# Strassen's seven products for the first product of a two-layer mixture, with both products interleaved

## The chip, the cores and the metric

The kernel runs on one core of one Trainium2 chip. The metric is the device time of one execution in microseconds, the median of several. Below, PE is the engine that does the matmuls (with PEld its weight loads), DVE the vector engine, ACT the scalar engine, POOL the GpSimd engine, and SP the engine whose queue issues most of the DMAs. L123 is line 123 of the kernel before.

## What is computed

The reference is float32 throughout: a gated linear attention, then a first mixture without routing, then a second one over E = 4 experts. N is 3072 tokens, the model width is 384, the hidden width F = 1024.

```
a = x @ w1;  b = x @ w2;  x1 = ((a * b) @ w3) @ w_out          # first mixture
p = probs / (probs.sum(-1, keepdims=True) + 1e-09)
for e in range(4):                                             # second mixture
    h = maximum(x1 @ W1[e], 0)                                 # first product,  384 -> 1024
    out += p[:, e:e+1] * (h @ W2[e])                           # second product, 1024 -> 384
```

The change is in the second mixture and in the loads that prepare it.

## The kernel before

**Float32 from three matmuls.** Each float32 operand is split into a high part, rounded to float32r, and a low part, the rest. `mm3` (L45) makes a product of three matmuls into one PSUM bank: high with high, low with high, high with low. The high part is an ACT copy, the low part a subtraction on POOL or DVE (`split`, L52).

**First stage (attention and first mixture).** A planner (`Plan`, L316) takes every piece of work with an engine, a cost, a due number and the pieces it depends on, and calls the pieces in the order of a modelled clock: of the pieces that are ready on an engine, the one with the lowest due number goes first. That gives each engine a fixed program order, and on the chip each engine works through its own in order. The planner knows only the dependencies it is told of. The tile framework adds the waits that buffers need: the first instruction that writes a new tile waits until the tile that had the slot before has been read for the last time, wherever these reads stand in the other engines' orders.

Eight token tiles of 384 go through the first mixture. For the last two tiles the PE's order is: x1 of tile 6 (72 matmuls, three results), then the products `a` and `b` of tile 7 (16 results, `products`, L633), then x1 of tile 7 (`moe`, L688). All these results use one pool of three PSUM banks (`pmm`, L415), in turn. An x1 result is copied out by ACT (`evac`, L733), an `a` result by ACT (`copy_a`, L654), a `b` result by DVE, which multiplies it with the copy of `a` (`mult`, L658). While tile 7 is at work, the planner also places the first weights of the second mixture: `opened` (L894) is the point at which the attention's memory is free, after the products of tile 6; from there eight loads `wload` (L865), with their splits on ACT and POOL, chained by explicit dependencies on the buffers they reuse.

**Second mixture.** After the planner, the order is written out by hand. For each expert e and each of six tiles of 512 tokens: for each of eight blocks f of 128 hidden units, nine matmuls of 512 columns (three blocks of the width, `mm3` each) make h in a PSUM bank (`hps`, four banks); ACT takes relu and the high part out of the bank, DVE the low part (L987, L988). One step later follow twelve matmuls of 384 columns (`outs`, L971: four groups of 128 tokens), which add this block's part of the second product to four accumulators in PSUM (`ops`). After the eighth block DVE adds p times the accumulators to `acc` in SBUF, and for the last expert they go to DRAM. Weight loads and the splits of x1 for the next tile (POOL) are generators in a list `side`; `tick` (L939) advances each by one step after each f. `check_words` (L120) is a test of the raw weights of the first mixture, with DMAs of about 1 MB and three ACT passes for each of 17 pieces.

Of the kernel before, what the change touches and what calls it, by code (L numbers as in the profile page):

```python
# [402 lines left out]
def gated_attention_moe_kernel(tc, qT, kT, aT, vP, w1, w2, w3T, wo, probs, ew, out):  # L403
# [4 lines left out]
    with tc.manual_schedule(), root:  # L408
# [216 lines left out]

        ab_done = {}
        x1_use = {}
        wts = {}
        conv_done = {}
        g_lo = {}  # L630
# [57 lines left out]
        def moe(j):  # L688
# [24 lines left out]
            for m, (d, f0, f1) in enumerate(((0, 0, 3), (0, 3, 6), (1, 0, 3), (1, 3, 6), (0, 6, 8), (1, 6, 8),  # L713
                                             (2, 0, 3), (2, 3, 6), (2, 6, 8))):
                def unit(d=d, f0=f0, f1=f1):
                    if f0 == 0:
                        us["x", d] = pmm.tile([128, 512], F32, tag="mm", name="xps")[:, :TT]
                    for f in range(f0, f1):
                        s = slice(d * 128, (d + 1) * 128)
                        gg = tiles["g", j, f]  # L720
                        mm3(nc, us["x", d], wts[2, 0][:, f, s], wts[2, 1][:, f, s], gg[:, 0], gg[:, 1],
                            f == 0, f == KF - 1)

                deps = [prev] + [g_lo[j, f] for f in range(f0, f1)]
                if f0 == 0:
                    slots[d] = []
                prev = add("PE", 3 * (f1 - f0) * MM, due + UNIT_DUE * (16 + m), unit, w3_done, deps,
                           bank=slots[d] if f0 == 0 else None)
                if d == KD - 1:
                    for f in range(f0, f1):  # L730
                        x1_use[j, f] = prev
                if f1 == KF:
                    def evac(d=d):  # L733
                        x1 = tiles["x1"]() if callable(tiles["x1"]) else tiles["x1"]
                        A.activation(out=x1[:, d, j * TT:(j + 1) * TT], in_=us["x", d], func=ACTF.Copy)  # L735
                    slots[d].append(add("ACT", act(TT), due + UNIT_DUE * (16 + m), evac, prev, pre_done))


        pre = []
# [117 lines left out]
        add("DVE", 1.0, 3 * TILE_DUE, norm_p, add("SP", 0.5, 2 * TILE_DUE, load_p))  # L857


        slots = {}  # L860
        n_raw = [0]
        wraw = []
        epool = None

        def wload(n):  # L865

            e, f = divmod(n, KF)
            slots[n] = []
            rs = []
            for u in range(2):  # L870
                r = wraw[n_raw[0] % len(wraw)]
                n_raw[0] += 1
                nc.sync.dma_start(out=r, in_=ew[u][e, f])
                if n % 12 < 8:
                    w = epool.tile([128, 2, TT], F32R, tag="ws", name="ws", bufs=16)
                else:
                    w = mpool.tile([128, 2, TT], F32R, tag="gg", name="wg", bufs=KF)
                slots[n].append(w)
                rs.append(r)
            yield  # L880
            yield
            for u in range(2):
                yield from split(nc, slots[n][u][:, 0], slots[n][u][:, 1], rs[u])

        def open_e():
            att_s.close()
            nonlocal epool
            epool = root.enter_context(tc.tile_pool(name="e", bufs=1, side="right"))
            t = mpool.tile([128, 6, TT], F32, tag="xt", name="wraw", bufs=2)
            wraw.extend(t[:, i] for i in range(6))  # L890

        att_all = [d for n in at.values() for d in n.values()]
        j = NTILE - 1
        opened = add("SP", 0.0, j * TILE_DUE, open_e, att_all, ab_done[j - 1])  # L894
        freed = []
        for n in range(8):
            due = j * TILE_DUE + WL_STEP * n
            gen = {}

            def step(n=n, gen=gen):  # L900
# [12 lines left out]
            freed.append(prev)  # L913

        xsb = []

        def xsplit(n):
            t = n % NT2
            return split(nc, xsb[n % 2][:, 0], xsb[n % 2][:, 1], x1[:, :, t * T2:(t + 1) * T2])

        def x_hi():
            xsb.extend(wtile([128, 2, KD, T2], F32R, "xs") for _ in range(2))
            tiles["xsplit"] = xsplit(0)
            next(tiles["xsplit"])

        def x_lo():
            finish(tiles["xsplit"])
# [5 lines left out]
        hb = wtile([128, 3, 2, T2], F32R, "hb")  # L933
        ps1.close()


        side = []

        def tick():  # L939
            for g in list(side):  # L940
                if next(g, side) is side:
                    side.remove(g)

        acc = [wtile([128, 8, DM], F32, "acc") for _ in range(NR // 8)]
        pho = root.enter_context(tc.tile_pool(name="ph", bufs=4, space=PSUM))
        poo = root.enter_context(tc.tile_pool(name="po", bufs=4, space=PSUM))
        wraw += [mpool.tile([128, TT], F32, tag=t, name="wraw", bufs=2) for t in "aagg"]
        n_raw = [0]
        late = list(range(8, 12))
# [4 lines left out]
        n_test = B * NCH  # L954

        def held_out():
            ps = pho.tile([128, T2], F32, tag="h", name="fps")[0:1, 0:1]
# [4 lines left out]
        nxt = 12  # L962
        nh = 0
        for e in range(E):
            for t in range(NT2):
                n = e * NT2 + t
                x = xsb[n % 2]
                ops_ = [poo.tile([128, 512], F32, tag="o", name="ops")[:, :DM] for _ in range(4)]
                hs = {}

                def outs(f):  # L971
                    w = slots[e * KF + f][1]
                    hh = hs.pop(f)
                    for m in range(4):
                        mm3(nc, ops_[m], hh[:, 0, m * 128:(m + 1) * 128], hh[:, 1, m * 128:(m + 1) * 128],
                            w[:, 0], w[:, 1], f == 0, f == KF - 1)

                for f in range(KF + 1):
                    if f < KF:
                        w = slots[e * KF + f][0]  # L980
                        ps = pho.tile([128, T2], F32, tag="h", name="hps")
                        for kk in range(KD):
                            mm3(nc, ps, w[:, 0, kk * 128:(kk + 1) * 128], w[:, 1, kk * 128:(kk + 1) * 128],
                                x[:, 0, kk], x[:, 1, kk], kk == 0, kk == KD - 1)
                        hh = hb[:, nh % 3]
                        nh += 1
                        A.activation(out=hh[:, 0], in_=ps, func=ACTF.Relu)  # L987
                        V.scalar_tensor_tensor(out=hh[:, 1], in0=ps, scalar=0.0, in1=f32(hh[:, 0]),  # L988
                                               op0=ALU.max, op1=ALU.subtract)
                        hs[f] = hh  # L990
                    if f:
                        outs(f - 1)
                        if t == NT2 - 1 and nxt < E * KF:
                            side.append(wload(nxt))
                            nxt += 1
                    if f == 3 and n + 1 < E * NT2:
                        side.append(xsplit(n + 1))
                    if late:
                        side.append(wload(late.pop(0)))
                    if f == 5 and n and tests:  # L1000
                        side.append(check_words(nc, *tests.pop(0), n_test, centre, w_reach, excess))
                        n_test += 1
                        if not tests:
                            n_held = n + 1
                    if f == 5 and not tests and n == n_held:
                        held_out()
                    tick()
                for m in range(4):
                    r = t * 4 + m
                    ac = acc[r // 8][:, r % 8]  # L1010
                    if e == 0:
                        V.tensor_scalar(out=ac, in0=ops_[m], scalar1=p_sb[:, r, e:e + 1], scalar2=None, op0=ALU.mult)
                    else:
                        V.scalar_tensor_tensor(out=ac, in0=ops_[m], scalar=p_sb[:, r, e:e + 1], in1=ac,
                                               op0=ALU.mult, op1=ALU.add)
                    if e == E - 1:
                        q = nc.scalar if t == NT2 - 1 else nc.sync
                        q.dma_start(out=out[r * 128:(r + 1) * 128], in_=ac)
# [68 lines left out]
```

## Time and profile before

| | |
|---|---|
| median of 3 runs | 1264.54 us (1264.09 to 1265.92) |
| the profiled execution | 1265.13 us, its span 1263.3 us |
| PE busy | 1227.6 us, 97% of the span, 8994 matmuls |
| DVE, ACT, POOL busy | 429.3, 416.5, 294.6 us |
| mean granted PE clock | 0.996 |

A matmul's duration in the trace is longer than the distance to the next one, because matmuls overlap in the array: what a matmul costs in a stream is the distance between starts. The second mixture begins at 452.05 us of the span. The granted clock is 1.00 at 2.4 GHz and 0.50 at 1.2 GHz.

### The profile page before, as it was taken

What the parts mean: (1) busy time and instruction counts of PE and PEld (TensorE: products, weight loads), DVE (VectorE), ACT (ScalarE), POOL (GpSimd) and SP (SyncE); (2) the same over time, 40 slices, a digit from 0 to 9 for tenths busy, and PEclk for the clock granted to TensorE, in tenths of its full rate; (3) what the DMA queues carried; (4) which work ended last, traced back from release to release, by engine and by line L of the source; (5) the groups of instructions that cost most, each with busy time, mean ns of one, the idle gap of its engine ahead of it and who ended that gap; (6) DMA issues with size and microseconds to landing.
All of it is one profiled execution on the core that took longest, in us unless ns stands there. A gap on an engine that the chain in (4) does not pass through costs nothing.

```text
span 1263.3 us, 21102 instructions
## 1 busy us (share of the span) xinstructions
PE 1227.6 (97%) x8994; PEld 1132.7 (90%) x8994; DVE 429.3 (34%) x718; ACT 416.5 (33%) x738; POOL 294.6 (23%) x228
## 2 busy tenths in 40 slices
PE   3899999999999999999999999999999999999997
PEld 2799999999999989999998989999999999899997
DVE  8788996223512112222222222212222222222222
ACT  5445445333322422322252332233232333111110
POOL 3332007543412552100161111133111122001110
PEclk9899999999999999999999999999999999999999
DMA  9746836422202120102121000221001210000000
GB/s 333 225 128 189 290 112 189 128 87 82 69 19 61 51 88 1 38 25 100 39 63 37 10 29 25 96 72 34 34 34 34 84 34 1 26 25 26 25 27 27
DMA packets 52360, 94.67 MB, mean 75 GB/s; under 512 B 8736, under 2 KB 29728, under 8 KB 52256
## 3 DMA queue, kind: packets, MB, share of 16 engines
q1 hardware_dynamic: 51680, 92.44, 22.8%
q8 instruction: 72, 1.18, 0.4%
q10 hardware_dynamic: 576, 0.79, 0.2%
q14 instruction: 32, 0.26, 0.1%
HBM read 79.84 MB, written 11.01 MB: 72 GB/s over the span
## 4 chain that ended last, share of the span: by engine, by line
PE 96%; DMA 2%; ACT 1%; DVE 0%; SPq 0%; issue 0%; DVEq 0%; ACTq 0%
PE ops L49 11%; PE ops L47 11%; PE hps L49 11%; PE ops L48 11%; PE hps L48 11%; PE hps L47 10%; PE abps L47 6%; PE abps L48 5%; PE abps L49 5%; PE xps L47 3%; PE xps L49 3%; PE xps L48 3%; DMA ra<-in_aT_dram 2%; PE yps L568 2%; PE su L542 1%; PE yps L592 1%
## 5 line engine op out<-in xcount | busy, mean ns | idle before, releaser
L988 DVE SCALAR_TENSOR_TENSOR hb<-hps,hb 128x512 fp32r<-128x512 f32 x192 | 133.0, 693 | 599.2 <-ACT hb L987 599.2
L987 ACT ACTIVATE hb<-hps 128x512 fp32r<-128x512 f32 x192 | 115.0, 599 | 575.3 <-PE hps L49 574.9
L56 POOL TENSOR_TENSOR xs<-x,xs 128x1536 fp32r<-128x1536 f32 x24 | 84.1, 3504 | 496.9 <-ACT xs L54 496.9
L49 PE MATMUL ops<-ws,hb 128*128 128x384 f32 x576 | 194.1, 337 | 0.0
L47 PE MATMUL ops<-ws,hb 128*128 128x384 f32 x576 | 193.8, 336 | 0.0
L48 PE MATMUL ops<-ws,hb 128*128 128x384 f32 x576 | 193.4, 336 | 0.0
L49 PE MATMUL hps<-xs,ws 128*128 128x512 f32 x432 | 170.6, 395 | 0.0
L48 PE MATMUL hps<-xs,ws 128*128 128x512 f32 x432 | 170.1, 394 | 0.0
L47 PE MATMUL hps<-xs,ws 128*128 128x512 f32 x432 | 168.4, 390 | 0.6 <-ACT x L735 0.6
L47 PEld LDWEIGHTS ops<-ws,hb 128*128 128x128 f32 x576 | 108.2, 188 | 5.5
L48 PEld LDWEIGHTS ops<-ws,hb 128*128 128x128 f32 x576 | 108.1, 188 | 5.4
L49 PEld LDWEIGHTS ops<-ws,hb 128*128 128x128 f32 x576 | 108.0, 188 | 0.0
L49 PEld LDWEIGHTS hps<-xs,ws 128*128 128x128 f32 x432 | 81.0, 187 | 17.5
L47 PEld LDWEIGHTS hps<-xs,ws 128*128 128x128 f32 x432 | 81.2, 188 | 14.3 <-ACT x L735 0.9
L48 PEld LDWEIGHTS hps<-xs,ws 128*128 128x128 f32 x432 | 81.0, 188 | 14.1
L660 DVE TENSOR_TENSOR g_sb<-abps,a_sb 128x384 f32<-128x384 f32 x64 | 35.5, 555 | 116.5 <-PE abps L49 107.8
L56 POOL TENSOR_TENSOR ws<-wraw,ws 128x384 fp32r<-128x384 f32 x48 | 47.9, 1018 | 86.8 <-ACT ws L54 86.8
L47 PE MATMUL abps<-xt,w2h 128*128 128x384 f32 x192 | 67.3, 351 | 0.0
L47 PE MATMUL abps<-xt,w1h 128*128 128x384 f32 x192 | 67.0, 349 | 0.0
L47 PE MATMUL ops<-wg,hb 128*128 128x384 f32 x192 | 65.0, 338 | 0.0
L49 PE MATMUL ops<-wg,hb 128*128 128x384 f32 x192 | 65.0, 338 | 0.0
L48 PE MATMUL ops<-wg,hb 128*128 128x384 f32 x192 | 65.0, 338 | 0.0
(116 smaller groups left out, 2192.6 us busy)
## 6 DMA issues: line engine op xcount, KB each, us to landing
wraw<-in_ew_dram SPq DMA_DIRECT2D x64, 192.0 KB, 3.9
c_raw<-in_w3T_dram SPq DMA_DIRECT2D x16, 512.0 KB, 4.6
w_raw<-in_w3T_dram SPq DMA_DIRECT2D x8, 1024.0 KB, 5.0
ra<-in_aT_dram SPq DMA_DIRECT2D x24, 260.0 KB, 3.9
c_raw<-in_w_dram SPq DMA_DIRECT2D x16, 384.0 KB, 6.0
rk<-in_kT_dram SPq DMA_DIRECT2D x24, 256.0 KB, 3.1
rq<-in_qT_dram SPq DMA_DIRECT2D x24, 256.0 KB, 3.7
rv<-in_vP_dram SPq DMA_DIRECT2D x24, 256.0 KB, 3.7
```

Source lines behind the costliest of these rows:

```text
L47: nc.tensor.matmul(out=ps, lhsT=lh, rhs=rh, start=first, stop=False)
L48: nc.tensor.matmul(out=ps, lhsT=ll, rhs=rh, start=False, stop=False)
L49: nc.tensor.matmul(out=ps, lhsT=lh, rhs=rl, start=False, stop=last)
L56: (lo_eng or nc.gpsimd).tensor_tensor(out=dst_lo, in0=src, in1=f32(dst_hi), op=ALU.subtract)
L542: PE.matmul(out=r["ups"][rows, t, p], lhsT=r["kT"][half, p, rows], rhs=v[half, p, g], start=True, stop=True)
L568: PE.matmul(out=r["y"][rows, p, t], lhsT=Z[rows, p], rhs=r["q"][rows, p, half], start=p == 0, stop=False)
L592: PE.matmul(out=r["y"][rows, p, t], lhsT=v[half, p, g], rhs=r["s"][half, g, p], start=first and t == 0 and p == 0, stop=p == NP - 1)
L660: V.tensor_tensor(out=us["g", f], in0=us[f, 1], in1=us["a", f], op=ALU.mult)
L987: A.activation(out=hh[:, 0], in_=ps, func=ACTF.Relu)
L988: V.scalar_tensor_tensor(out=hh[:, 1], in0=ps, scalar=0.0, in1=f32(hh[:, 0]), op0=ALU.max, op1=ALU.subtract)
```

## The change

The first product is done for pairs: a pair of hidden blocks (k, so that f is 2k and 2k + 1), a pair of halves of a token tile that is now 768 tokens (halves of 384), and the first two of the three blocks of the model width. For these 2 x 2 x 2 blocks, seven products with sums of weight blocks and sums of x1 blocks take the place of eight (Winograd's form); the third block of the width is added with four ordinary products, into the same banks where that is possible. So one pair ("quad" below) has eleven products of 3 matmuls of 384 columns, in seven groups, each group one PSUM bank. The results are combined after the PE: seven additions on DVE that read PSUM, one copy on ACT, four relus on ACT and four low parts on DVE, now all from SBUF. There are 4 experts x 4 tiles x 4 pairs = 64 quads.

`load_a` loads the W1 blocks of a pair, forms the five weight sums on POOL and splits ten blocks at once; `load_b` loads a W2 block and splits it with DVE. The x1 sums are made on DVE when the first expert reaches a tile (`x_sums`), nine operands of a tile are split into twelve slots, kept in DRAM as well (`x_keep`), and read back and split again for the other experts (`x_load`). The second product of a quad is interleaved with the first product of the next one: after each group of seven, the PE does `share[g]` of twelve pieces, each piece one `mm3`. PSUM is split into two banks for groups and six accumulators. The accumulated output overwrites x1.

```diff
-T2 = 512
+HT = 384
+T2 = 2 * HT
+KP = KF // 2
+NOP = 9
...
+        groups = (((0, 0),), ((7, 1),), ((1, 2), (2, 6)), ((3, 3),), ((6, 4), (5, 8)), ((4, 5), (5, 6)),
+                  ((8, 7), (9, 8)))
+        wa, wb = {}, {}
...
+        def load_a(e, k):
+
+            w = wa[e, k] = epool.tile([128, 2, 10, 128], F32R, tag="wa", name="wa", bufs=KP)
+            a = epool.tile([128, 10, 128], F32, tag="raw", name="araw", bufs=1)
             for u in range(2):
+                nc.sync.dma_start(out=a[:, 3 * u:3 * u + 3], in_=ew[0][e, 2 * k + u].rearrange("p (n t) -> p n t", n=KD))
             yield
             yield
+            for dst, x, y, op in ((6, 3, 4, ALU.add), (7, 6, 0, ALU.subtract), (8, 1, 7, ALU.subtract),
+                                  (3, 0, 3, ALU.subtract), (9, 2, 5, ALU.subtract)):
+                G.tensor_tensor(out=a[:, dst], in0=a[:, x], in1=a[:, y], op=op)
+            yield
+            A.activation(out=w[:, 0], in_=a, func=ACTF.Copy)
+            yield
+            V.tensor_tensor(out=w[:, 1], in0=a, in1=f32(w[:, 0]), op=ALU.subtract)
+
+        def load_b(e, f):
+
+            w = wb[e, f] = mpool.tile([128, 2, DM], F32R, tag="gg", name="wb", bufs=KF)
+            r = mpool.tile([128, DM], F32, tag="ag"[f % 2], name="braw", bufs=2)
+            nc.sync.dma_start(out=r, in_=ew[1][e, f])
+            yield
+            yield
+            yield from split(nc, w[:, 0], w[:, 1], r, V)
...
+        def x_sums(t):
+
+            t1, t2, t3, t4 = (sums[:, n] for n in range(4))
+            V.tensor_tensor(out=t1, in0=block(t, 0, 1), in1=block(t, 0, 0), op=ALU.subtract)
+            V.tensor_tensor(out=t2, in0=block(t, 1, 1), in1=t1, op=ALU.subtract)
+            V.tensor_tensor(out=t3, in0=block(t, 1, 1), in1=block(t, 0, 1), op=ALU.subtract)
+            V.tensor_tensor(out=t4, in0=block(t, 1, 0), in1=t2, op=ALU.subtract)
...
+        def x_keep(t, o):
+            nc.sync.dma_start(out=kept[t, o], in_=x_src(t, o))
+
+        def x_load(n, o):
+
+            x = x_slot(n, o)
+            nc.sync.dma_start(out=f32(x[:, 1]), in_=kept[n % NT2, o])
+            for _ in range(3):
+                yield
+            A.activation(out=x[:, 0], in_=f32(x[:, 1]), func=ACTF.Copy)
+            yield
+            V.tensor_tensor(out=x[:, 1], in0=f32(x[:, 1]), in1=f32(x[:, 0]), op=ALU.subtract)
...
-        freed = []
-        for n in range(8):
-            due = j * TILE_DUE + WL_STEP * n
+        for k in range(KP):
...
-                    gen["g"] = wload(n)
+                    gen["g"] = load_a(0, k)
...
-            prev = add("SP", 2 * 0.55, due, step, opened, freed[n - 3] if n > 2 else None, freed[n - 1] if n else None)
-            def act0(step=step):
+            def step2(step=step):
                 step()
                 step()
 
-            prev = add("ACT", act(TT), due + 2, act0, prev)
-            prev = add("POOL", pool(TT) + act(TT), due + 2, step, prev)
-            prev = add("POOL", pool(TT), due + 2, step, prev)
-            freed.append(prev)
...
-        x_h = add("ACT", 1.36, j * TILE_DUE + XS_DUE, x_hi, ab_done[j])
-        add("POOL", 3.4, j * TILE_DUE + XS_DUE, x_lo, x_h)
+            prev = add("SP", 2 * 0.55, due, step, opened)
+            prev = add("POOL", 5 * pool(128), due + 2, step2, prev)
+            prev = add("ACT", act(1280), due + 2, step, prev)
+            add("DVE", dve(1280), due + 2, step, prev)
...
+        s_done = add("DVE", 4 * dve(HT), j * TILE_DUE + XS_DUE, lambda: x_sums(0), opened, x_done)
+        x_ready = add("ACT", 0.0, j * TILE_DUE + XS_DUE, x_open, ab_done[j])
+        for o in range(NOP):
+            h = add("ACT", act(HT), j * TILE_DUE + XS_DUE + o, lambda o=o: x_hi(0, o), x_ready, s_done)
+            add("DVE", dve(HT), j * TILE_DUE + XS_DUE + o, lambda o=o: x_lo(0, o), h)
...
-        pho = root.enter_context(tc.tile_pool(name="ph", bufs=4, space=PSUM))
-        poo = root.enter_context(tc.tile_pool(name="po", bufs=4, space=PSUM))
+        pho = root.enter_context(tc.tile_pool(name="ph", bufs=2, space=PSUM))
+        poo = root.enter_context(tc.tile_pool(name="po", bufs=6, space=PSUM))
...
+        side = [load_b(0, f) for f in range(KF)]
...
+        for o in range(NOP):
+            x_keep(0, o)
+        tick(side)
...
+        order = [(0, 0), (0, 1), (0, 2), (1, 0), (1, 1), (1, 2), (1, 3), (1, 4), (1, 5), (0, 3), (0, 4), (0, 5)]
+        share = (2, 2, 1, 2, 2, 1, 2)
...
+        def second(q, fi, m):
+            e, t, k, h = q
...
+            hh, w = h[fi, m // 3][0], wb[e, 2 * k + fi]
+            tok = slice(m % 3 * 128, (m % 3 + 1) * 128)
+            first, last = (fi == m // 3, fi != m // 3)
+            mm3(nc, ps, hh[:, 0, tok], hh[:, 1, tok], w[:, 0], w[:, 1], k == 0 and first, k == KP - 1 and last)
...
+            for g, parts in enumerate(groups):
+                ps = pho.tile([128, 512], F32, tag="h", name="hps")[:, :HT]
+                for m, (a, o) in enumerate(parts):
+                    w, x = wa[e, k], xo[n, o]
+                    mm3(nc, ps, w[:, 0, a], w[:, 1, a], x[:, 0], x[:, 1], m == 0, m == len(parts) - 1)
+                if g == 0:
+                    A.activation(out=c1, in_=ps, func=ACTF.Copy)
                     if late:
+                        relu_lo(late)
+                elif g == 1:
+                    add_to(u2, ps, c1)
+                elif g == 2:
+                    add_to(hq[0, 0][1], ps, c1)
+                    relu_hi(hq[0, 0])
+                elif g == 3:
+                    add_to(u3, ps, u2)
+                    relu_lo(hq[0, 0])
+                elif g == 4:
+                    add_to(w5, ps, u2)
+                    add_to(hq[1, 1][1], ps, u3)
+                    relu_hi(hq[1, 1])
+                elif g == 5:
+                    add_to(hq[1, 0][1], ps, u3)
+                    relu_hi(hq[1, 0])
+                    relu_lo(hq[1, 1])
+                else:
+                    add_to(hq[0, 1][1], ps, w5)
+                    relu_hi(hq[0, 1])
+                    relu_lo(hq[1, 0])
+                    late = hq[0, 1]
+                for _ in range(share[g]):
+                    if todo:
+                        second(before, *todo.pop(0))
...
+                if g == 1 and t == NT2 - 1 and e + 1 < E and k:
+                    side.append(load_a(e + 1, k - 1))
+                if g == 1 and t == 0 and e and not k:
+                    side.append(load_a(e, KP - 1))
+                if g == 3 and e + 1 < E and t == NT2 - 1 and k > 1:
+                    side.extend(load_b(e + 1, 2 * (k - 2) + u) for u in range(2))
+                if g == 3 and e and t == 0 and k < 2:
+                    side.extend(load_b(e, 2 * (k + 2) + u) for u in range(2))
+                tick(side)
+                tick(loads)
+
+                if n + 1 < E * NT2:
+                    if k == KP - 1:
+                        ops = (3,) if g == 0 else (g + 3,) if g < 6 else ()
                     else:
+                        ops = (g - 1,) if k == KP - 2 and 0 < g < 4 else ()
+                    for o in ops:
+                        if n + 1 < NT2:
+                            x_hi(t + 1, o)
+                            x_lo(t + 1, o)
+                            x_keep(t + 1, o)
+                        else:
+                            loads.append(x_load(n + 1, o))
+                            tick(loads[-1:])
...
+        relu_lo(late)
+        for fi, m in order:
+            second(before, fi, m)
```

## Rows read from the trace of the kernel before

**Rows 1.** The page: busy time by engine, then the chain that ended last, by engine.
```profile
PE 1227.6 (97%) x8994; PEld 1132.7 (90%) x8994; DVE 429.3 (34%) x718; ACT 416.5 (33%) x738; POOL 294.6 (23%) x228
...
PE 96%; DMA 2%; ACT 1%; DVE 0%; SPq 0%; issue 0%; DVEq 0%; ACTq 0%
```
**Rows 2.** Windows: x1 of tile 6; products of tile 7; x1 of tile 7; second mixture.
```profile
401.30:413.90 12.60, 12.60 (x74) 12.60 (x74) 0.56 (x1) 3.27 (x7) 4.97 (x5) 1.00 0.46 141
413.90:438.70 24.80, 24.80 (x145) 24.80 (x144) 3.90 (x7) 11.35 (x24) 13.27 (x14) 1.00 0.20 56
438.70:452.05 13.35, 12.77 (x74) 12.44 (x72) 0.56 (x1) 4.96 (x10) 10.09 (x8) 1.00 0.21 57
452.05:1256.40 804.35, 804.18 (x4034) 728.15 (x4034) 185.45 (x290) 224.84 (x331) 128.33 (x71) 1.00 0.12 39
```
**Rows 3.** Timeline of PE: first matmul of each of three neighbouring streams.
```profile
801.56 0.39 PE L47 MATMUL hps<-xs,ws 128*128 128x512 f32 x1
...
803.64 0.34 PE L47 MATMUL ops<-wg,hb 128*128 128x384 f32 x1
...
805.73 0.39 PE L47 MATMUL hps<-xs,ws 128*128 128x512 f32 x1
```
**Rows 4.** Groups by line: matmuls of the first product on one of mm3's three lines.
```profile
L47 PE MATMUL hps<-xs,ws 128*128 128x512 f32 x432 | 168.4, 390 | 0.6 <-ACT x L735 0.6
...
L47 PE MATMUL hps<-xs,wg 128*128 128x512 f32 x144 | 56.8, 395 | 0.0
```
**Rows 5.** Groups by line and shape: durations on DVE, ACT and POOL.
```profile
L56 POOL TENSOR_TENSOR xs<-x,xs 128x1536 fp32r<-128x1536 f32 x24 | 84.1, 3504 | 496.9 <-ACT xs L54 496.9
L56 POOL TENSOR_TENSOR ws<-wraw,ws 128x384 fp32r<-128x384 f32 x48 | 47.9, 1018 | 86.8 <-ACT ws L54 86.8
L1014 DVE SCALAR_TENSOR_TENSOR acc<-ops,p_sb,acc 128x384 f32<-128x384 f32 x72 | 39.6, 612 | 23.6 <-PE ops L49 23.6
L660 DVE TENSOR_TENSOR g_sb<-abps,a_sb 128x384 f32<-128x384 f32 x64 | 35.5, 555 | 116.5 <-PE abps L49 107.8 <-ACT a_sb L656 4.0 <-ACT u L482 1.9
L54 ACT ACTIVATE xs<-x 128x1536 fp32r<-128x1536 f32 x24 | 35.5, 1479 | 0.0
L54 ACT ACTIVATE ws<-wraw 128x384 fp32r<-128x384 f32 x48 | 22.9, 515 | 1.4 <-DMA wraw<-in_ew_dram 1.4
L56 DVE TENSOR_TENSOR t<-c_m,t 128x512 fp32r<-128x512 f32 x16 | 11.8, 737 | 1.2 <-ACT t L54 1.1
L56 DVE TENSOR_TENSOR w1l<-c_m,w1h 128x384 fp32r<-128x384 f32 x8 | 5.1, 641 | 2.1 <-ACT w1h L54 2.1
```
**Rows 6.** Timeline of ACT around x1 of tile 6 and the first product of tile 7.
```profile
404.14 0.94 ACT L54 ACTIVATE ws<-wraw 128x384 fp32r<-128x384 f32 x2 [1.43 <-DMA wraw<-in_ew_dram]
408.77 0.49 ACT L735 ACTIVATE x<-xps 128x384 f32<-128x384 f32 x1 [3.69 <-PE xps L49]
...
413.97 0.49 ACT L735 ACTIVATE x<-xps 128x384 f32<-128x384 f32 x1 [2.84 <-PE xps L49]
415.59 0.49 ACT L656 ACTIVATE a_sb<-abps 128x384 f32<-128x384 f32 x1 [1.13 <-PE abps L49]
```
**Rows 7.** The weight loads of the second mixture: SP's timeline, and the tile's DMAs.
```profile
401.48 51.00 SPq L873 DMA_DIRECT2D wraw<-in_ew_dram  x24
```
```profile
DMA to landing us min/median/max: 2.2/2.6/4.1
```
**Rows 8.** Windows early in the span: PE busy (third figure) and granted clock (third from the end).
```profile
36.00:38.00 2.00, 0.20 (x16) 0.06 (x4) 1.26 (x2) 1.55 (x4) 0.79 (x1) 1.00 0.98 80
...
39.00:40.00 1.00, 0.21 (x16) 0.07 (x7) 0.65 (x3) 0.02 (x1) 0.00 (x0) 0.56 0.66 226
...
45.00:46.00 1.00, 1.00 (x46) 0.99 (x43) 0.48 (x2) 0.29 (x1) 0.57 (x1) 0.53 0.24 40
46.00:47.00 1.00, 1.00 (x24) 0.93 (x17) 0.54 (x2) 0.26 (x1) 0.62 (x1) 1.00 0.64 127
```
**Rows 9.** Timeline of PE: the first matmul of the second mixture.
```profile
452.05 0.50 PE L47 MATMUL hps<-xs,ws 128*128 128x512 f32 x1 [0.58 <-ACT x L735]
```
**Rows 10.** DMA issues of the page: one form of the check loads.
```profile
w_raw<-in_w3T_dram SPq DMA_DIRECT2D x8, 1024.0 KB, 5.0
```

More of the change, by code (lines that the diff above doesn't have):

```diff
@@ new lines, in gated_attention_moe_kernel, with block @@
+        kept = tc.dram_tile((NT2, NOP, 128, HT), F32, name="kept")
+        def block(t, k, h):
+            return tiles["x1"][:, k, t * T2 + h * HT:t * T2 + (h + 1) * HT]
+        def x_sums(t):
[4 more added lines that the diff above has]
+            V.tensor_tensor(out=t4, in0=block(t, 1, 0), in1=t2, op=ALU.subtract)
@@ new lines, in x_slot, with x_src, x_hi, x_lo @@
+        def x_slot(n, o):
+            xo[n, o] = xslots[(n * NOP + o) % len(xslots)]
+            return xo[n, o]
+        def x_src(t, o):
+            return (block(t, 0, 0), sums[:, 1], block(t, 1, 0), sums[:, 2], sums[:, 0], sums[:, 3],
+                    block(t, 2, 0), block(t, 1, 1), block(t, 2, 1))[o]
+        def x_hi(t, o):
+            A.activation(out=x_slot(t, o)[:, 0], in_=x_src(t, o), func=ACTF.Copy)
+        def x_lo(t, o):
+            V.tensor_tensor(out=xo[t, o][:, 1], in0=x_src(t, o), in1=f32(xo[t, o][:, 0]), op=ALU.subtract)
@@ L888, in open_e @@
             epool = root.enter_context(tc.tile_pool(name="e", bufs=1, side="right"))
-            t = mpool.tile([128, 6, TT], F32, tag="xt", name="wraw", bufs=2)
-            wraw.extend(t[:, i] for i in range(6))
+            sums = mpool.tile([128, 6, HT], F32, tag="xt", name="sums", bufs=2)
         att_all = [d for n in at.values() for d in n.values()]
@@ L926, in x_lo, with x_open @@
-        def x_lo():
-            finish(tiles["xsplit"])
-        x_h = add("ACT", 1.36, j * TILE_DUE + XS_DUE, x_hi, ab_done[j])
-        add("POOL", 3.4, j * TILE_DUE + XS_DUE, x_lo, x_h)
+            prev = add("SP", 2 * 0.55, due, step, opened)
+            prev = add("POOL", 5 * pool(128), due + 2, step2, prev)
+            prev = add("ACT", act(1280), due + 2, step, prev)
+            add("DVE", dve(1280), due + 2, step, prev)
+        def x_open():
+            for _ in range(3):
+                x = wtile([128, 4, 2, HT], F32R, "xo")
+                xslots.extend(x[:, n] for n in range(4))
@@ L934, in gated_attention_moe_kernel @@
+        hslots = [h[:, n] for h in ht for n in range(4)]
+        tmp = wtile([128, 8, HT], F32, "tmp")
         ps1.close()
[L937 to L944, printed above, removed]
-        pho = root.enter_context(tc.tile_pool(name="ph", bufs=4, space=PSUM))
-        poo = root.enter_context(tc.tile_pool(name="po", bufs=4, space=PSUM))
@@ L953, in gated_attention_moe_kernel @@
         tests += [(w_flat, w3T[f]) for f in range(KF)]
[L954 removed]
         def held_out():
[L957 removed]
+            ps = pho.tile([128, 512], F32, tag="h", name="fps")[0:1, 0:1]
             V.tensor_reduce(out=over, in_=excess, axis=mybir.AxisListType.X, op=ALU.add)
@@ L960, in held_out @@
             V.tensor_scalar(out=held, in0=ps, scalar1=0.0, scalar2=None, op0=ALU.is_le)
[L962 to L997, printed above, removed]
-                    if late:
[L999 to L1012, printed above, removed]
-                    else:
[L1014 to L1018, printed above, removed]
@@ new lines, in checks, with tick @@
+        def checks():
+            for n, (w, src) in enumerate(tests):
+                gen = check_words(nc, w, src, B * NCH + n, centre, w_reach, excess)
+                next(gen)
+                next(gen)
+                yield
+                for _ in gen:
+                    yield
+            held_out()
+        checking = checks()
+        side = [load_b(0, f) for f in range(KF)]
+        loads = []
+        def tick(some):
+            for g in list(some):
+                if next(g, some) is some:
+                    some.remove(g)
@@ new lines, in gated_attention_moe_kernel @@
+        for o in range(NOP):
[3 more added lines that the diff above has]
+        share = (2, 2, 1, 2, 2, 1, 2)
+        accs = {}
+        def second(q, fi, m):
+            e, t, k, h = q
+            if (e, t, m) not in accs:
+                accs[e, t, m] = poo.tile([128, 512], F32, tag="o", name="ops")[:, :DM]
+            ps = accs[e, t, m]
+            hh, w = h[fi, m // 3][0], wb[e, 2 * k + fi]
+            tok = slice(m % 3 * 128, (m % 3 + 1) * 128)
+            first, last = (fi == m // 3, fi != m // 3)
+            mm3(nc, ps, hh[:, 0, tok], hh[:, 1, tok], w[:, 0], w[:, 1], k == 0 and first, k == KP - 1 and last)
+            if k < KP - 1 or not last:
+                return
+            r = t * 6 + m
+            ac = tiles["x1"][:, m // 2, t * T2 + m % 2 * DM:t * T2 + (m % 2 + 1) * DM]
+            if e == 0:
+                V.tensor_scalar(out=ac, in0=ps, scalar1=p_sb[:, r, e:e + 1], scalar2=None, op0=ALU.mult)
+            else:
+                V.scalar_tensor_tensor(out=ac, in0=ps, scalar=p_sb[:, r, e:e + 1], in1=ac, op0=ALU.mult, op1=ALU.add)
+            if e == E - 1:
+                (nc.scalar if t == NT2 - 1 else nc.sync).dma_start(out=out[r * 128:(r + 1) * 128], in_=ac)
```

64 lines of the change are left out of this document (32 added, 32 removed).

## The prediction

> **What bounds the kernel now.** I read the page first: the PE is busy for 97% of the span and is 96% of the chain that ended last [rows 1]. So a change pays by what it takes from the PE's stream, and costs by what it makes the PE wait for. Next the windows by stage: in the second mixture the PE works for 804.18 of 804.35 us, at full clock, while DVE is busy for 185 and POOL for 128 us [rows 2]. All that the change can save lies in this window. In the two windows before it, tile 7's products and its x1, the PE is just as full (24.80 of 24.80), and there the change puts other loads. The reader should see that there is no slack anywhere: each wait that the change adds lengthens the run.
>
> **What the PE saves.** Starts of neighbouring streams give the cost of a matmul: nine of 512 columns take 803.64 - 801.56 = 2.08 us, 0.2311 each; twelve of 384 take 805.73 - 803.64 = 2.09 us, 0.1742 each [rows 3]. The first product has (432 + 144) x 3 = 1728 matmuls [rows 4], the second 24 x 8 x 12 = 2304. 1728 x 0.2311 + 2304 x 0.1742 = 800.7 us, close to the window's 804.35. After the change the first product has 64 quads x 33 = 2112 matmuls of 384 columns, 367.9 us instead of 399.4: **31.5 us saved**. The second product keeps its 2304. A quad is then 69 x 0.1742 = 12.02 us of PE.
>
> **Cost 1: one raw buffer in the last tile of the first stage.** The four `load_a` of expert 0 hang on `opened` alone, and share one buffer `araw`; the planner is not told of that. With a negative WL_STEP, k = 3 has the lowest due number, so all four DMAs go to SP in the order 3, 2, 1, 0. In the planner's clock (its costs settle the order only) POOL's five additions cost 2.11, so the blocks follow each other every 2 to 4 us: ACT's order becomes x1 copy d=0, block 3, copy d=1, block 2, copy d=2, block 1, `copy_a` of f=0, block 0, `copy_a` of f=1; DVE's 3, 2, 1, `mult` 0, block 0, `mult` 1. On the chip the DMA of the next block must wait until DVE has read the last one.
>
> One block takes: DMA, 2.66 us (first issue 401.48, ACT began with such a pair at 404.14 [rows 6, 7]); five additions of 128 columns on POOL, 2.2 (from 1018 ns at 384 and 3504 at 1536 columns, 2.16 ns a column, so 0.46 each, slightly overlapped [rows 5]; bounds 1.0 and 5 x 1.018); ACT with 1280 columns 1.27 (between 515 and 1479 ns); DVE with 1280 columns 1.5 (from 737 at 512 and 641 or less at 384; bounds 1.2 and 2.1); handovers 0.4. Together 8.0.
>
> The chain: block 3 is on POOL until 406.4, on ACT after the x1 copy of 408.77 until 410.5, off DVE at 412.05. Block 2: DMA to 414.9, POOL 417.1, ACT 418.45, DVE 420.0. The x1 copy d=2, which stood at 413.97, is queued behind it on ACT: 418.9. Its bank is wanted by the third product of tile 7, which would start at 413.90 + 18 x 0.1742 = 417.05 and starts at 419.0. **Wait 1.95.** Block 1: ACT until 426.45, DVE 428.0. Behind it on ACT stands `copy_a` of f=0 (415.59 before [rows 6]): 426.9; the fourth product wants its bank at 420.55. **Wait 6.4.** Block 0: ACT until 434.45, and behind it `copy_a` of f=1, 434.9; the sixth product wants that bank at 430.2. **Wait 4.75.** `mult` 1 behind block 0 on DVE adds 0.15. After that no load is left. Where the sixth group began, the PE is 13.4 us later than before; the products then flow on. With POOL's bounds 9 to 22.
>
> The splits of the first x1 operands (nine on ACT, nine on DVE) start when tile 7's products end and have the 12.5 us of its x1; nine times 0.5 us hide there, and put ACT's last split of tile 7 some 4 us later, just when the PE wants it: at most 0.3, counted as nothing. Were that cover gone, they would cost 4.5.
>
> **Cost 2: the first quad.** `side` holds eight `load_b`; their raw tiles have four slots (two of each tag), so W2 blocks 4 to 7 are loaded only when DVE has read blocks 0 to 3. ACT's eight copies are placed together after group 1, DVE's eight low parts after group 2's addition. With T the first matmul of the quad (which has no second product to fill it, 33 x 0.1742 = 5.75 us): DVE does group 2's addition at 2.7 to 3.25 (0.555 [rows 5]), low part 0 until 3.85; then the DMA of block 4, 2.2 to 2.6 us to landing [rows 7], so ACT copies it at 6.6; blocks 5 to 7 follow until ACT is free at 8.7 and DVE at 9.4. Only behind them stand ACT's relu of h and DVE's addition of group 3. Group 5 wants group 3's bank (two banks) at 4.35 and gets it at about 10. Then the last two additions on DVE hold the last group for 0.6: the quad ends at 12.7 instead of 5.75, **7.0 us**. Bounds: 0, if the loads land early, and 9 with the longest landing of 4.1.
>
> **The clock.** Early in the span the PE did 0.20 us of work in 2 us, and the granted clock fell to 0.50 (the lower level, 1.2 GHz) during 39 to 40, and was back at 1.00 by 46 [rows 8]: up to 7 us at half, so at most 3.5 us lost for a drop. Of that kind are the waits of 6.4, 4.75 and 5.7 us. After the first, what runs slowly is two products, whose delay lies inside the next wait: I take 1 for the last tile, and 2.5 for the first quad, whose matmuls after the wait run on. The Trainium skill has a rule for it ("TensorE: Matmul & The Clock Gate", HAM oscillation): bursts of matmuls separated by waits for data are throttled again each time, so each wait would cost its own drop. By that rule the clock would cost 10.5 instead of 3.5. The trace agrees with the drop, but no run shows it after each of several waits.
>
> **Cost 3: the quads in their flow.** DVE has seven additions of 0.555 and four low parts of about 0.55 (SBUF, 384 columns), 6.1 of 12.02 us; a tile adds nine low parts and six accumulations of 0.612 [rows 5], which makes 11.3 in the first quad of a tile. A group's bank is wanted again 1.5 to 2.4 us after the group ends; the addition needs 0.3 + 0.555: some 1.2 us of cover in each group, enough for one side job of 0.6 or one of 1.5 with a small rest. If the cover is gone, a quad loses the whole excess, 0.3 us or more. Where an expert changes, ACT must wait in order for a `load_a` whose DMAs stand on SP behind a check load of 1 MB (5.0 us to landing [rows 10]): in four quads, 0.7 each, so 2.5. The last test, with its matmul in one of the two group banks, 0.5. Keeping and reloading nine operands a tile is 144 DMAs of 192 KB over some 770 us; each x operand has three groups (4.7 us) until ACT wants it, against 2.2 to 4.1 [rows 7]: nothing. The hand-over at 452.05, a 0.58 us wait for the last x1 copy [rows 9], stays, and so does the tail, where three accumulations follow the last matmuls as four do now.
>
> **Sum.** 1265.1 (the profiled execution) - 31.5 + 13.4 + 1 + 7.0 + 2.5 + 2.5 + 0.5 = 1260.4. The median of the runs before is 0.6 below the profiled execution, so **1260**.
>
> **The rivals.**
> - *No stall in the last tile* (order or buffers let the blocks pass): cost 1 and its clock fall away, 1260 - 14.4 = 1245.5. For it: eight chained loads pass today without a wait. Against it: the buffer is one, and the next DMA can't start before DVE's read. 0.13.
> - *Neither entry costs much*: also without cost 2, 1236. Four of eight raw tiles do have slots. 0.07.
> - *The other side: two banks for groups.* If DVE falls behind by more than its cover in every quad, the PE waits in each. It decides from 4.5 / 63 = 0.07 us a quad; at 0.3 us it is 19 us, 1279. For it: four banks served this purpose before, and side jobs are now on DVE. Against it: DVE is idle for half of a quad. 0.12.
> - *Heavier expert changes*: `load_a`, `load_b`, reloaded operands and accumulations in the same two quads, 3 us more at three changes: 1269. 0.11.
> - *The clock falls after each wait*, unhidden: 7 us more, 1267. The Trainium skill's page named above would have it so. 0.10.
> - My forecast, both entry waits and a flow at the PE's rate: 0.47, by itself 1254 to 1266.
>
> **Numbers.** The range takes in the forecast, the first rival and those at 1267 and 1269, and leaves out those at 1236 and 1279: 1243 to 1274. A measurement of this kernel tells about 0.2% (2.5 us). Faster, below 1262.0: 0.31 of the forecast's 0.47, the two at 1245 and 1236, and 0.04 of the others, 0.55. Same: 0.13 of the forecast and 0.06 of the rivals, 0.19. Slower: 0.26.
>
> **What would show it.** After: 2112 matmuls of the first product, 384 columns, 0.174 apart; PE waits in tile 7's products for ACT's x1 copy and `copy_a`, about 2, 6.4 and 4.8 us, with ACT waiting for POOL and SP for DVE; the second mixture starting near 466; one wait of 5 to 6 us for DVE in the first quad; a lower clock after these. A quad in the flow of 12.0 us proves the saving, one of 12.1 or more the two-bank rival. The prediction is wrong if the PE's order in tile 7 shows no waits, or if waits of DVE return in every quad.

## The result and the profile after

The change makes the kernel slower by 0.9%: a median of 1275.47 us (1273.18 to 1278.14, 4 runs) against 1264.32 us (4 runs), a ratio of 1.0087 with a 95% interval of 1.0062 to 1.0111. The prediction was 1260, with a range up to 1274 and more chance for faster than for slower. The profiled execution took 1273.97 us, 8.8 more than that of before, so the sums below are made against 8.8.

The page after, with busy time by engine and the chain that ended last, which answers to [rows 1]:

```profile
PE 1213.5 (95%) x9378; PEld 1189.5 (93%) x9378; DVE 772.1 (61%) x1438; ACT 495.8 (39%) x970; POOL 186.8 (15%) x220
...
PE 87%; DMA 3%; DVE 3%; ACT 2%; POOL 1%; issue 1%; SPq 1%; ACTq 0%; POOLq 0%; DVEq 0%
```

The PE is 14 us less busy, and the run is longer all the same: the chain that sets the end now leaves the PE for 13% of the span, for DMA, DVE, ACT and POOL. So the time went into waits. The windows by stage (start:end, length, busy us of PE, PEld, DVE, ACT, POOL, granted clock, DMA share, GB/s) answer to [rows 2]:

```profile
400.50:412.96 12.46, 12.46 (x73) 12.46 (x73) 4.83 (x6) 2.56 (x4) 3.88 (x6) 1.00 0.16 47
412.96:453.93 40.97, 31.30 (x145) 30.05 (x145) 8.20 (x10) 12.15 (x22) 14.16 (x22) 0.79 0.21 73
453.93:467.44 13.51, 12.93 (x75) 12.61 (x73) 5.59 (x10) 4.81 (x12) 1.17 (x1) 1.00 0.16 45
467.44:1265.68 798.24, 782.50 (x4418) 778.95 (x4418) 514.89 (x992) 303.74 (x567) 30.41 (x60) 0.99 0.23 75
```

Tile 7's products take 40.97 us instead of 24.80, of which 9.7 us are idle PE and 6.5 us matmuls at a lower clock. The second mixture, which the change was to shorten, takes 798.24 instead of 804.35 us: of a saving of about 30 us only 6 arrive. Who kept the PE waiting is in the chart of waits from tile 7's products to the end (us in total, times, longest; the lines marked as left out lie before it or are the hand-over of 0.6 us that the kernel before has too):

```profile
PE hps L50 <- DVE tmp L1052: 14.5, 5, 6.3
PE abps L50 <- ACT a_sb L660: 7.6, 2, 5.4
...
PE abps L50 <- ACT x L739: 2.0, 1, 2.0
...
PE fps L997 <- DVE small L996: 1.0, 1, 1.0
```

Three of these nine waits lie in tile 7's products and six in the quads; apart from these six the quads run evenly. Starts of two neighbouring quads in the PE's timeline, and the start and end of the longest quad:

```profile
531.41 0.34 PE L50 MATMUL hps<-xo,wa 128*128 128x384 f32 x1
...
543.53 0.34 PE L50 MATMUL hps<-xo,wa 128*128 128x384 f32 x1
...
862.34 0.45 PE L50 MATMUL hps<-xo,wa 128*128 128x384 f32 x1
...
880.43 0.34 PE L50 MATMUL hps<-xo,wa 128*128 128x384 f32 x1
```

A quad of 69 matmuls takes 12.12 us, 0.1757 each, and 56 of the 63 distances between quads lie within 0.01 us of that. The seven others, read from the same timeline: the first two quads take 15.00 and 12.62, quads 14, 17, 32 and 47 (counted from 0) 13.76, 14.16, 18.09 and 13.75, quad 52 13.50. This is nearly the whole difference: the flow is 64 x 12.12 = 775.7 us, 28.7 less than 804.35; the second mixture starts at 467.44 instead of 452.05 (+15.4); the first quad, which has 33 matmuls of 0.1757 = 5.80 us, and the second cost +9.7; quads 14, 17, 32, 47 cost +11.3, quad 52 (the last test) +1.4; the end after the last matmul is 0.5 shorter. -28.7 + 15.4 + 9.7 + 11.3 + 1.4 - 0.5 = 8.6, of 8.8.

**The last tile.** ACT's timeline of after, beside [rows 6]:

```profile
408.35 1.26 ACT L886 ACTIVATE wa<-araw 128x1280 fp32r<-128x1280 f32 x1
409.52 0.48 ACT L739 ACTIVATE x<-xps 128x384 f32<-128x384 f32 x1
416.57 1.27 ACT L886 ACTIVATE wa<-araw 128x1280 fp32r<-128x1280 f32 x1 [6.58 <-POOL araw L884]
417.75 0.47 ACT L739 ACTIVATE x<-xps 128x384 f32<-128x384 f32 x1
424.84 1.27 ACT L886 ACTIVATE wa<-araw 128x1280 fp32r<-128x1280 f32 x1 [6.62 <-POOL araw L884]
426.02 0.47 ACT L660 ACTIVATE a_sb<-abps 128x384 f32<-128x384 f32 x1
433.15 1.27 ACT L886 ACTIVATE wa<-araw 128x1280 fp32r<-128x1280 f32 x1 [6.66 <-POOL araw L884]
434.33 0.47 ACT L660 ACTIVATE a_sb<-abps 128x384 f32<-128x384 f32 x1
```

The order is the forecast one: each copy that the PE needs stands right behind a block that comes 8.3 us after the block before it, and ACT idles 6.6 us ahead of each.

**An expert change.** In quad 13 SP issues a check load of 1.15 MB and right behind it two W1 blocks. Rows of the timelines of SP, POOL, ACT and DVE, and the PE's wait that ends the row of events (of the four W1 loads in SP's row two belong to quad 13, the others to quad 14):

```profile
631.00 0.38 SPq L128 DMA_DIRECT2D w_raw<-in_w_dram  x1
631.43 12.50 SPq L879 DMA_DIRECT2D araw<-in_ew_dram  x4
```
```profile
637.70 2.56 POOL L884 TENSOR_TENSOR araw<-araw 128x128 f32<-128x128 f32 x5 [179.19 <-DMA araw<-in_ew_dram]
```
```profile
640.30 1.27 ACT L886 ACTIVATE wa<-araw 128x1280 fp32r<-128x1280 f32 x1 [2.77 <-POOL araw L884]
```
```profile
641.61 1.49 DVE L888 TENSOR_TENSOR wa<-araw,wa 128x1280 fp32r<-128x1280 f32 x1 [2.49 <-ACT wa L886]
643.02 0.55 DVE L1052 TENSOR_TENSOR tmp<-hps,tmp 128x384 f32<-128x384 f32 x1
```
```profile
643.62 0.44 PE L50 MATMUL hps<-xo,wa 128*128 128x384 f32 x1 [1.38 <-DVE tmp L1052]
```

The blocks are in POOL's hands 6.3 us after SP issued the first of them (they landed 5.6 to 5.7 us after their issue, where the median of all W1 blocks is 2.6). ACT waits for POOL, DVE for ACT, the addition that gives a bank back to the PE starts at 643.02, and the PE goes on at 643.62.

### The profile page after: what moved, and what is told of

It is laid out like the page before. It is cut to its first block, busy times and chain, and to the rows that moved or that the text cites. A ratio compares the mean times of both kernels' runs of the same rounds, so it can differ in the third digit from the quotient of the medians.

```text
span 1272.2 us, 23227 instructions
## 1 busy us (share of the span) xinstructions
PE 1213.5 (95%) x9378; PEld 1189.5 (93%) x9378; DVE 772.1 (61%) x1438; ACT 495.8 (39%) x970; POOL 186.8 (15%) x220
## 3 DMA queue, kind: packets, MB, share of 16 engines
HBM read 101.07 MB, written 18.09 MB: 94 GB/s over the span
## 4 chain that ended last, share of the span: by engine, by line
PE 87%; DMA 3%; DVE 3%; ACT 2%; POOL 1%; issue 1%; SPq 1%; ACTq 0%; POOLq 0%; DVEq 0%
PE ops L50 10%; PE ops L51 10%; PE ops L52 10%; PE hps L50 9%; PE hps L51 9%; PE hps L52 9%; PE abps L50 5%; PE abps L51 5%; PE abps L52 5%; PE xps L50 3%; PE xps L52 2%; PE xps L51 2%; DMA araw<-in_ew_dram 2%; PE yps L571 2%; POOL araw L884 1%
## 5 line engine op out<-in xcount | busy, mean ns | idle before, releaser
L1052 DVE TENSOR_TENSOR tmp<-hps,tmp 128x384 f32<-128x384 f32 x448 | 243.2, 555 | 246.5 <-PE hps L52 224.7
L1055 ACT ACTIVATE ht<-tmp 128x384 fp32r<-128x384 f32 x256 | 134.4, 525 | 444.6 <-DVE tmp L1052 444.6
L50 PE MATMUL ops<-wb,ht 128*128 128x384 f32 x768 | 261.2, 340 | 0.0
L51 PE MATMUL ops<-wb,ht 128*128 128x384 f32 x768 | 260.9, 340 | 0.0
L52 PE MATMUL ops<-wb,ht 128*128 128x384 f32 x768 | 260.9, 340 | 0.0
L50 PE MATMUL hps<-xo,wa 128*128 128x384 f32 x704 | 239.3, 340 | 15.3 <-DVE tmp L1052 14.5
L51 PE MATMUL hps<-xo,wa 128*128 128x384 f32 x704 | 237.8, 338 | 0.0
L52 PE MATMUL hps<-xo,wa 128*128 128x384 f32 x704 | 237.4, 337 | 0.0
L50 PEld LDWEIGHTS hps<-xo,wa 128*128 128x128 f32 x704 | 133.2, 189 | 18.6 <-DVE tmp L1052 17.2
L50 PEld LDWEIGHTS ops<-wb,ht 128*128 128x128 f32 x768 | 144.7, 188 | 0.0
L52 PEld LDWEIGHTS ops<-wb,ht 128*128 128x128 f32 x768 | 144.4, 188 | 0.0
L51 PEld LDWEIGHTS ops<-wb,ht 128*128 128x128 f32 x768 | 144.2, 188 | 0.0
L1058 DVE SCALAR_TENSOR_TENSOR ht<-tmp,ht 128x384 fp32r<-128x384 f32 x256 | 141.9, 554 | 2.4
L51 PEld LDWEIGHTS hps<-xo,wa 128*128 128x128 f32 x704 | 133.2, 189 | 0.0
L52 PEld LDWEIGHTS hps<-xo,wa 128*128 128x128 f32 x704 | 133.1, 189 | 0.0
L664 DVE TENSOR_TENSOR g_sb<-abps,a_sb 128x384 f32<-128x384 f32 x64 | 35.5, 554 | 97.5 <-PE abps L52 76.8
L50 PE MATMUL abps<-xt,w2h 128*128 128x384 f32 x192 | 68.3, 356 | 7.6 <-ACT a_sb L660 7.6
L50 PE MATMUL abps<-xt,w1h 128*128 128x384 f32 x192 | 68.6, 357 | 2.1 <-ACT x L739 2.0
L52 PE MATMUL abps<-xt,w1h 128*128 128x384 f32 x192 | 66.0, 344 | 0.0
L51 PE MATMUL abps<-xt,w1l 128*128 128x384 f32 x192 | 66.0, 344 | 0.0
L52 PE MATMUL abps<-xt,w2h 128*128 128x384 f32 x192 | 65.5, 341 | 0.0
```

The source lines that it names most:

```text
L50: nc.tensor.matmul(out=ps, lhsT=lh, rhs=rh, start=first, stop=False)
L51: nc.tensor.matmul(out=ps, lhsT=ll, rhs=rh, start=False, stop=False)
L52: nc.tensor.matmul(out=ps, lhsT=lh, rhs=rl, start=False, stop=last)
L664: V.tensor_tensor(out=us["g", f], in0=us[f, 1], in1=us["a", f], op=ALU.mult)
L1052: V.tensor_tensor(out=dst, in0=ps, in1=x, op=ALU.add)
L1055: A.activation(out=h[0][:, 0], in_=h[1], func=ACTF.Relu)
```

## The experiments

**The planner is told of the raw buffer.**

```diff
+        freed = None
         for k in range(KP):
...
-            prev = add("SP", 2 * 0.55, due, step, opened)
+            prev = add("SP", 2 * 0.55, due, step, opened, freed)
...
-            add("DVE", dve(1280), due + 2, step, prev)
+            freed = add("DVE", dve(1280), due + 2, step, prev)
```

> The planner is told that the four first loads of W1 share one raw buffer (each load depends on DVE's read of the one before); the work is the same. Theory (engines blocked in order by pieces whose data cannot have come yet): ACT's copies no longer stand behind a late block, the PE's waits of 2.0, 5.4 and 2.2 us in tile 7's products go, and the second mixture starts at 452 to 453 us of the span instead of 467.4; the run is 15 us shorter than the 1275.5 of the change, 1260. Rival (the loads' own work on POOL, ACT and DVE delays the copies): the work stays, the waits stay in part, start later than 458, 1266 or more.

1258.62 us; the ratio to the kernel before, run again beside the experiments, is 0.9949 (0.9933 to 0.9966), where the change has 1.0087, so 1.4% or 17 us shorter. No wait of tile 7's products is left, and the second mixture starts at 450.63:

```profile
450.63 0.45 PE L50 MATMUL hps<-xo,wa 128*128 128x384 f32 x1 [0.58 <-ACT x L739]
```

The four loads and all their work are still there; only their places in the engines' orders differ. The rival falls: the work by itself costs the PE no wait here.

**Half of the W2 blocks later.**

```diff
-        side = [load_b(0, f) for f in range(KF)]
+        side = [load_b(0, f) for f in range(KF // 2)]
...
-                if g == 3 and e and t == 0 and k < 2:
+                if g == 3 and t == 0 and k < 2:
```

> Only W2 blocks 0 to 3 are started ahead of the first quad, blocks 4 to 7 in the first two quads as for the other experts. Theory (ACT and DVE stand in order before splits of blocks whose raw slots are not free yet): the wait of 6.3 us in the first quad goes, the quad takes 7 instead of 15.0 us, the run is 8 us shorter than the 1275.5 of the change, 1267.5. Rival (a quad without a second product is bound by the chain of DVE's additions through two banks): the quad still takes 11 us or more, 1272 or more.

1268.63 us, ratio 1.0029 (1.0013 to 1.0045), 0.6% or 7 us less than the change. The first quad takes 8.30 us, the second 12.11: 7.2 us less together.

```profile
469.60 0.45 PE L50 MATMUL hps<-xo,wa 128*128 128x384 f32 x1 [0.58 <-ACT x L739]
...
477.90 0.33 PE L50 MATMUL hps<-xo,wa 128*128 128x384 f32 x1
```

A rest of the rival is true: without a second product one wait for DVE of 1.0 us stays in the first quad, which is 2.5 us above its 5.80.

**Checks apart from the W1 loads.**

```diff
-                if g == 0 and i > 0:
+                if (g == 0 and i > 0 or g == 4 and e == E - 1 and t) and not (calls % 3 == 0 and (e, t, k) in weight_quads):
                     next(checking, None)
+                    calls += 1
```

`weight_quads` are the twelve quads with a `load_a`; every third call issues a check load. When a load is due in such a quad, the checks stop until these quads are past, so their ACT passes leave them as well.

> No check load of about 1 MB is issued in the four quads around an expert change in which W1 is loaded; the last checks are made up for by a second step in the quads of the last expert. Theory (a W1 load queued behind a check load lands late, and ACT, then DVE wait for it in order): the four long quads (13.76, 14.16, 18.09 and 13.75 us instead of 12.12) become 12.1 to 12.4, the run is 11 us shorter than the 1275.5 of the change, 1264.5. Rival (DVE has more work than time in the quads after an expert change): they stay above 13 us, 1272 or more.

1264.32 us, ratio 0.9981 (0.9971 to 0.9991), 1.1% or 13 us less than the change by the ratios, 11 by the medians. All quads are at 12.12 but the first two and the one with the last test. Of the five waits for DVE one is left, that of the first quad:

```profile
PE hps L50 <- DVE tmp L1052: 6.3, 1, 6.3
```

The edit alone doesn't tell the load from the ACT passes. The trace of the change does: ahead of the late split ACT was idle for 2.77 us and waited for POOL, and POOL waited for the DMA.

**The three edits together.**

> The three edits (chained W1 loads, W2 blocks 4 to 7 later, checks apart from expert changes) together. Theory: three separate waits in three places, so the gains add: 15 + 8 + 11 = 34 us, 1241.5, 1.8% below the kernel before, and the granted clock stays at 1.00 through the second mixture. Rival (the flow of the quads loses what the entry gives, by two banks or by DVE): 1252 or more.

1239.94 us (1238.70 to 1243.83), ratio 0.9805 (0.9788 to 0.9821): faster than both kernels, by 1.9% and 2.8%. The three gains add up: 34.8 us by the medians, for 35.5 measured. The chart of waits in the second mixture:

```profile
PE hps L50 <- DVE tmp L1053: 1.0, 1, 1.0
PE fps L998 <- DVE small L997: 0.9, 1, 0.9
...
PE hps L50 <- ACT x L739: 0.6, 1, 0.6
```

and the windows of tile 7's products (with a little on either side) and of the second mixture, at a granted clock of 1.00:

```profile
412.00:438.00 26.00, 26.00 (x152) 26.00 (x151) 8.29 (x10) 11.57 (x20) 15.35 (x22) 1.00 0.36 117
...
451.94:1231.65 779.71, 777.47 (x4418) 775.50 (x4418) 514.16 (x992) 302.70 (x567) 30.51 (x60) 1.00 0.24 76
```

The second mixture is 24.6 us shorter than before; that is what the new form is worth here with these waits gone; the first quad (8.30 us) and the last test keep a rest.

**A twelfth product.**

```diff
-        groups = (((0, 0),), ((7, 1),), ...
+        groups = (((0, 0), (0, 0)), ((7, 1),), ...
```

> Built on the kernel with all three edits (1239.9): the first group of each quad does its product twice, so a quad has twelve products as it would without Strassen's form; the sum in that bank, and so the output, is changed by it. Theory (the flow of the quads is the PE's stream and nothing else): a quad takes 12.12 x 72 / 69 = 12.65 us, the run is 64 x 0.53 = 34 us longer, 1274. Rival (waits through two banks or DVE have a share in the 12.12): part of the added product is hidden, 1265 or less.

1272.44 us, 32.5 more than with the three edits; a quad takes 12.64.

```profile
574.40 0.34 PE L50 MATMUL hps<-xo,wa 128*128 128x384 f32 x1
...
587.04 0.34 PE L50 MATMUL hps<-xo,wa 128*128 128x384 f32 x1
```

So the flow is the PE's stream: a product of three matmuls costs its full 0.52 us, and next to nothing of it is hidden. With twelve products this layout would be at 1.0057 (1.0039 to 1.0075) of the kernel before: all of the gain is the product left out.

**DVE's low parts made twice.**

```diff
                     relu_lo(hq[0, 0])
+                    relu_lo(hq[0, 0])
```

(the same at the other three places)

> Built on the kernel with all three edits (1239.9): each of the four low parts that DVE makes in a quad (about 0.55 us each) is made twice, with the same values, so DVE has 8.3 instead of 6.1 us of work in a plain quad. Theory (about 1.2 us of cover in each group): plain quads stay at 12.12, only the first quads of tiles, where accumulations and low parts of x1 come on top (13.5 us of DVE work), grow by up to 0.6: 1240 to 1248. Rival (the two group banks leave no cover): plain quads grow by 0.3 us or more, 1259 or more.

1259.28 us. Plain quads stay at 12.12, so at each of the four places there is room for 0.55 us more on DVE; whether the cover is the 1.2 us of the theory was not tried. The first quads of tiles, where it expected growth, stay at 12.12 too, away from an expert change. But the quads on either side of an expert change, nine in all, grow by 1.4 to 3.8 us, 19.1 us together, nearly all of the loss of 19.3; quads 0 and 2 grow by 0.6 and 0.8. Neither theory had this: the total is the rival's, the place is not.

```profile
PE hps L50 <- DVE tmp L1053: 9.1, 10, 1.3
PE hps L52 <- DVE xo L940: 5.5, 3, 1.9
```

## Why the prediction was wrong, point by point

**The saving**: predicted 31.5 us, measured 28.7. The matmul of 384 columns was sized from one stretch of twelve at 0.1742; over whole quads it is 0.1757. The window of before had said so: 804.35 us for a sum of 800.7. That window of the whole stage [rows 2] should have set the price.

**Cost 1, the raw buffer**: right in mechanism, order and total, not in how the total is made up. Predicted waits 1.95, 6.4 and 4.75 us, measured 2.0, 5.4 and 2.3, because products between the waits ran at the lower clock and filled part of the time. These 9.7 us of idle PE and 6.5 us of lower clock are 16.2, and since tile 7's products began 0.94 us earlier in this execution (412.96), the second mixture starts 15.4 us later, for 14.4 predicted. ACT's order alone sets the start of the sixth product: it came at 434.86, 14.2 us late. The forecast of 13.4 was reckoned from a start at 413.90; from 412.96 it is 14.3. Only the clock behind this last wait comes on top, 2 us where 1 was forecast (the last 11 products took 19.1 us, and 17.05 at the pace of [rows 2]). Telling the planner removes all of it, which shows the cause.

**Cost 2, the first quad**: predicted 9.5, measured 9.7, with a wait of 6.3 for 5.7. Loading four blocks later shows the cause of 7.2 of it. The other 2.5 stay then, with a wait of 1.0 for DVE; of these the working had only the 0.6 of the last group, so that the total came so close is partly luck.

**The clock**: windows (same columns, the granted clock third from the end) around waits of the PE, in tile 7's products, in the first quad, and in quads 14, 17 and 32:

```profile
419.00:420.00 1.00, 1.00 (x4) 1.00 (x4) 0.37 (x1) 0.00 (x0) 0.00 (x0) 0.50 0.00 0
420.00:428.00 8.00, 2.62 (x9) 2.11 (x9) 1.86 (x2) 1.65 (x2) 2.18 (x5) 0.50 0.16 49
434.00:435.00 1.00, 0.14 (x1) 0.15 (x2) 0.55 (x1) 1.00 (x3) 0.00 (x0) 1.00 0.88 329
436.00:437.00 1.00, 1.00 (x5) 1.00 (x4) 0.41 (x1) 0.53 (x1) 0.81 (x1) 0.50 0.00 0
...
479.00:485.00 6.00, 6.00 (x24) 6.00 (x23) 3.38 (x7) 1.97 (x4) 0.00 (x0) 0.62 0.06 22
```
```profile
640.00:660.00 20.00, 18.62 (x106) 18.30 (x105) 13.82 (x24) 11.34 (x19) 3.62 (x9) 1.00 0.38 119
680.00:700.00 20.00, 18.45 (x104) 17.94 (x103) 13.22 (x25) 7.49 (x15) 0.00 (x0) 1.00 0.01 2
860.00:880.00 20.00, 15.95 (x82) 15.46 (x81) 14.32 (x27) 10.99 (x20) 5.37 (x10) 0.91 0.38 122
```

In tile 7's products the clock was at the lower level (0.50) within 1 us of the PE's return from the wait of 2.0 us and through the wait of 5.4 us, was back at 1.00 by 434, in the wait of 2.3 us, and fell again behind it. It was at the lower level after the wait of 6.3 us in the first quad, fell 1 us after the return from the wait of 4.1 us, and stayed at 1.00 after those of 1.4 and 1.6 us. The rule of the Trainium skill that the prediction weighed ("TensorE: Matmul & The Clock Gate", HAM oscillation) says that bursts of matmuls separated by waits for data are throttled again each time. The trace agrees for the waits of 2.0, 2.3, 4.1 and 6.3 us (that of 5.4 found the clock already low), and not for those of 1.4 and 1.6. The rival that priced the rule at 7 us did not come: in the last tile 2 us came on top for 1, and the first quad with its clock is within 0.2 us of the forecast.

**Cost 3, the step that failed**: "in four quads, 0.7 each, so 2.5". The place was right: the check loads of quads 13, 16, 31 and 46 meet the W1 loads, and the loss shows in the quad after each. The size was wrong: 1.64, 2.04, 5.97 and 1.63 us, 11.3 together. The prediction gives no working for 0.7 (and four times 0.7 are 2.8); it names the check load's 5.0 us and not what comes after: POOL's five additions (2.6 us), ACT's 1.27 and DVE's 1.49 stand in line behind the late landing. A second term stood at nothing: the reloaded x1 operands, with 4.7 us of time against 2.2 to 4.1 to landing. In quad 31 they stand behind a check load too. They landed 6.4 to 6.5 us after their issue, and ACT idled for one of them before it could wait for the W1 block:

```profile
860.70 0.52 ACT L938 ACTIVATE xo<-xo 128x384 fp32r<-128x384 f32 x1 [4.95 <-DMA xo<-kept]
```

So the PE waits 4.1 us at once in quad 32, and the clock falls. The landing times of [rows 7] are those of the first 24 of the 64 weight loads, issued by 452 us. For the other 40, in the second mixture of the kernel before (460 to 1256 us), the same view says:

```profile
DMA to landing us min/median/max: 2.1/4.9/6.7
```

These were the loads to price by. Separating the checks from the W1 loads removes all four losses, so DVE's load at the change is not the cause; but doubling its low parts shows that it is close to being the next.

**The rivals**: two banks for groups lose nothing in the flow. By the sign that the prediction gave, a quad of 12.1 us or more, the measured 12.12 would speak for them; but no wait for DVE stands in those quads, 69 matmuls at 0.1757 are 12.12, and with a twelfth product 72 at 0.1757 are 12.65, for a measured 12.64. The sign was set on a matmul priced too low. The two rivals without the waits of the entry fell, for both waits are in the trace. "Heavier expert changes" came out at its price, 8.8 us beyond the forecast for 9, but not by its mechanism: it blamed the work that meets in the same quads, and with the checks moved away all of that work stays and the loss is gone. That its price fits is luck. The last test cost 1.4 for 0.5. Sum of the misses: 2.8 (the saving) + 1.0 (cost 1) + 0.2 (cost 2) + 8.8 (cost 3) + 0.9 (the last test) - 0.5 (the end) = 13.2, of the 13.6 us between the 1260.4 worked out and the 1273.97 of the profiled execution.

Not tried: raw buffers of their own for the four blocks, and moving only the check loads while their ACT passes stay.

## What to carry to other kernels

When work is moved into an engine's fixed order, ask for each piece when its data can be there at the earliest, and what the same engine has to do for the bottleneck right behind it: a planner that does not know of a shared buffer puts late pieces in front of urgent ones. The loss (15.4 us here) is not the pieces' own work, which cost the PE no wait in its better place. Price a delayed load with the whole line behind it (every engine that handles it in order), not with its transfer alone, and take its landing time from the stretch in which it will run. And take the price of a stream from the window of the whole stage; a few matmuls read from a timeline are 1% off, which here was a tenth of the gain.

## What the runs showed of the hardware

A pair of W1 blocks (192 KB each) landed 5.6 to 5.7 us after its issue right behind a 1.15 MB load on the same queue, and POOL had it 6.3 us after the first issue; the median of all W1 blocks was 2.6 us. The five additions of 128 columns on POOL took 2.3 to 3.3 us. Matmuls of 384 columns in the quads started 0.1757 us apart. The length of a wait alone did not settle whether the clock fell: after waits of 1.9 and 2.0 us in the run with the planner told, it stayed at 1.00 (windows 666.4:672 and 1038.4:1044), and after two of 1.9 us in the run with doubled low parts it was 0.63 and 0.61 (650.4:655 and 1050.6:1055). Why was not tried.
